# Heads paired as they lie in a fused RWKV and balanced-expert kernel

## The chip, the cores and the metric

The kernel runs on one core of a Trainium2 chip. The metric is device time in microseconds (us), the median of several runs. Before the change it is 385.69 us (three runs, 384.68 to 386.14).

The engines are named as in the profile: PE is TensorE's matmul stream and PEld its weight loads, DVE is VectorE, ACT is ScalarE, POOL is GpSimd, SP is SyncE, which here only issues DMAs.

## The reference

Two blocks run one after the other. The first is an RWKV attention with a decayed state, for 4 batches, 8 heads, 768 steps and 48 dimensions a head:

```
for t in range(S):
    cur = einsum('bhd,bhe->bhde', u * k[t], v[t])
    y[t] = einsum('bhd,bhde->bhe', r[t], state + cur)
    state = w * state + einsum('bhd,bhe->bhde', k[t], v[t])
```

Its output, 3072 tokens of 384 values, goes into a balanced mixture of eight experts. Token and expert pairs are taken in descending order of `x @ w_gate`; each token goes to one expert and each expert takes exactly 384 tokens. Then `out = relu(x @ w1[e]) @ w2[e]`.

## The kernel before

**Rounds.** `Mild.run` (L642) does the attention in 24 rounds. A round n is one batch (B = 4) and one chunk of 128 steps (6 chunks), for all eight heads. Rounds 0 to 3 are the first chunk and have no incoming state; rounds 20 to 23 are the last and leave none. The order on every engine is the order in which the code is written (a manual schedule), so an engine that waits holds up all that stands behind it in its queue.

**What a round does.** k, r and v are loaded by SP (`load`, L331) into rings of five (`krs`) and six (`vts`) slots; k and r come five rounds ahead. In round n:

- `turn(n + 2)`: TensorE transposes k and r of a later round, two heads at a time, into the PSUM banks tagged kT_ps and rT_ps, and VectorE scales them by powers of w into `krT` (L499).
- `own(n + 3)`, `own_sum`, `diagonal(n + 2)`: GpSimd multiplies r, k and u (`rk`), VectorE sums each head to `dd` (L450), ScalarE writes eight diagonal blocks `AT` (L509).
- `pairs(n + 1)`: TensorE forms the products of k and r (`g_ps`, one bank), VectorE places the lower triangle into AT (L526). This is what frees `g_ps`. The text calls it the placing.
- `keep`: TensorE forms the chunk's contribution to the state in the bank "counts" (`kv_ps`, L538), VectorE adds it (L543 or L546), GpSimd decays it (L544). GpSimd's `keys` (L438) makes the keys for it.
- `outputs(n)`: TensorE adds state and chunk parts in `y_ps` (L559), ScalarE copies it to x (L578). In rounds 4, 8, 12, 16 and 20 `gate` and `logits` form four rounds' expert logits, in the bank "few".
- `rows(n - 2)` or `rows_turned` and `rows_out`: x is transposed back to token rows, ScalarE copies them to `xr`, and SP writes them to `x_rows`. `rows` (L621) does eight small transposes into two banks, "few" and "counts"; `rows_turned` (L602) four larger ones into one bank.

**Heads in pairs.** The transposed operands stack two heads on 128 partitions, z = 0 and z = 1. `outputs` puts head h at partition half `h % 2` of its result, so that rows come out in order. Heads 0 to 3 go as (0,1) and (2,3). Heads 4 to 7 go as (5,6) and (7,4): a head of half z then has its result in the other half. For the pair (7,4) to lie side by side, head 4 is copied behind head 7 in `krs`, by `again_one` on ScalarE (L346, two copies a round for rounds 0 to 7) or `again` on VectorE (L342, one for rounds 8 to 23).

**After the rounds.** From round 17 on the early search (`Assignment.early`) runs in eleven steps between the rounds, by a list `steps` of round and place: it picks one expert from the logits of four chunks, then of the fifth, and lists 256 of its tokens (`list_ps`, L1461). GpSimd gathers them (L1550), and TensorE starts with their expert (`e_xT_ps`, `e_h_ps`, `e_o_ps`) while VectorE searches the tokens of the next. Then come the other experts, one after the other. The banks "few" and "counts" belong to the search and are lent to the rounds.

Of the kernel before, what the change touches and what calls it, by code (L numbers as in the profile page):

```python
# [23 lines left out]
T = 128  # L24
PD = 64
# [251 lines left out]
class Mild:  # L277
# [20 lines left out]
    def head(self, a, z):  # L298
        h = 2 * a + z
        return h if h < self.HP else self.HP + (h - self.HP + 1) % self.HP  # L300

    def open(self, ctx):
# [6 lines left out]
        self.krs = const.tile([128, self.NK, 2, H + 2, PD], F32, name="krs")  # L309
# [18 lines left out]
        self.xts, self.live, self.lgs = {}, {}, {}  # L328

    def load(self, n, what):  # L330
# [4 lines left out]
        for x in what:  # L335
            t = self.vts[:, n % self.NV] if x == "v" else self.krs[:, n % self.NK, "kr".index(x)]
            src = {"k": self.k, "r": self.r, "v": self.v}[x]
            nc.sync.dma_start(t[:, 0:H, 0:D], src[b, :, ts(c, T), :].rearrange("h s d -> s h d"))

    def again(self, n):  # L340
        kr, HP, H, D = self.krs[:, n % self.NK], self.HP, self.H, self.D
        self.nc.vector.tensor_copy(kr[:, :, H, 0:D], kr[:, :, HP, 0:D])  # L342

    def again_one(self, n, x):
        t, HP, H, D = self.krs[:, n % self.NK, x], self.HP, self.H, self.D
        self.nc.scalar.copy(t[:, H, 0:D], t[:, HP, 0:D])  # L346

    def start(self):
        nc, HP, H, D = self.nc, self.HP, self.H, self.D
        half = HP // 2  # L350
        nc.vector.memset(self.wp, 1.0)
        with nc.allow_non_contiguous_dma(reason="a row to the partitions"):
            for eng, z, aa, hh in ((nc.sync, 0, slice(0, half), slice(0, HP, 2)),
                                   (nc.scalar, 1, slice(0, half), slice(1, HP, 2)),
                                   (nc.sync, 0, slice(half, HP), slice(HP + 1, H, 2)),
                                   (nc.scalar, 1, slice(half, HP - 1), slice(HP + 2, HP + 3)),
                                   (nc.scalar, 1, slice(HP - 1, HP), slice(HP, HP + 1))):
                eng.dma_start(self.wp[z * PD:z * PD + D, aa], self.w[hh].rearrange("h d -> d h"))
# [17 lines left out]
        nc.gpsimd.memset(self.states, 0.0)  # L376
# [18 lines left out]
        nc.vector.reciprocal(AB[:, 1], AB[:, 0])  # L395
        for x, eng in ((0, nc.gpsimd), (1, nc.vector)):
# [7 lines left out]
    def gate_weights(self):  # L404
        for z in range(2):
            self.nc.sync.dma_start(self.wgp[z * PD:z * PD + self.D, :, 0:self.E],
                                     self.wg.rearrange("(a z d) e -> z d a e", z=2, d=self.D)[z])
# [39 lines left out]

# [80 lines left out]
    def keep(self, n):  # L528
# [3 lines left out]
        if c < C - 1:  # L532
# [9 lines left out]
            if c > 0:  # L542
                nc.vector.tensor_add(S, S, kv)  # L543
                nc.gpsimd.tensor_mul(S, S, wc)  # L544
# [3 lines left out]
    def outputs(self, n, between=None, last=lambda: None):  # L548
# [8 lines left out]
        def add(h, lhsT, rhs, stop):  # L557
            o, q = h // 2, h % 2
# [43 lines left out]
    def rows_turned(self, ns, tag, between=lambda: None):  # L602
        nc, HP = self.nc, self.HP
        shape = [128, len(ns), HP, T]
        ps = (self.walk.ps if tag == "few" else self.ps).tile(shape, F32, name="x_ps", tag=tag)
# [1492 lines left out]
```

## Time and profile before

| what | value |
|---|---|
| median of three runs | 385.69 us |
| the profiled execution's own time | 386.26 us |
| its span, first to last instruction | 384.4 us |
| mean granted clock of TensorE | 0.988 |
| busy: PE, DVE, ACT, POOL | 365.3, 286.8, 180.4, 140.5 us |
| round 5's turn starts | 39.63 us |
| the early expert's first transposes start | 125.45 us |
| first matmul of the next expert | 151.51 us |

All lines come from the profiled execution; times count from the start of its span. A line of the order of time gives start, duration, engine, source line, operation, output and inputs, shapes, and how many instructions were merged. A bracket gives the idle time just before it and what ended that. The granted clock is a share of full speed. A releaser is inferred: where several semaphores were waited for, the profile names one that came late, which need not be the one that the instruction depends on.

### The profile page before, as it was taken

The numbers are of one execution on the slowest core, as the hardware profiler recorded it, in microseconds if no ns is written. First come the engines' busy times: TensorE is split into PE (matmuls) and PEld (weight loads), VectorE is DVE, ScalarE is ACT, GpSimd is POOL, SyncE is SP. The second block draws the span as 40 slices with busy tenths as digits, with TensorE's granted clock in tenths as the row PEclk, the third lists the DMA queues.
The fourth block names the chain that finished last, engine by engine and source line by source line (L and its number), as shares of the span: only waits on it lengthen the run. The fifth ranks groups of instructions, "written<-read, shape, count | busy, mean of one in ns | idle before, by whom it ended". The sixth has DMA issues, their size and how long they took to land. (4 is left out here: it accounts for less than half of the span.)

```text
span 384.4 us, 10425 instructions
## 1 busy us (share of the span) xinstructions
PE 365.3 (95%) x4025; PEld 303.1 (79%) x4025; DVE 286.8 (75%) x963; ACT 180.4 (47%) x470; POOL 140.5 (37%) x174
## 2 busy tenths in 40 slices
PE   8879999999988999999999999999999999999994
PEld 7667878888867765677899799658756989989994
DVE  6875899798995677979679878869457974995730
ACT  4884879878762312225344444322222435535230
POOL 7991999877752004032131231202312213051031
PEclk9997999999999999999999999999999999999998
DMA  7997579987682156474282391507407676391110
GB/s 141 208 188 175 119 169 204 195 186 173 150 322 89 56 179 241 144 260 82 90 341 49 89 377 22 104 2 275 157 20 248 208 211 236 66 366 42 24 62 30
DMA packets 108138, 60.55 MB, mean 158 GB/s; under 512 B 90032, under 2 KB 102320, under 8 KB 108080
## 3 DMA queue, kind: packets, MB, share of 16 engines
q1 hardware_dynamic: 104736, 50.35, 47.9%
q0 software_dynamic: 3104, 9.44, 7.1%
q8 instruction: 34, 0.56, 0.6%
q14 instruction: 24, 0.20, 0.2%
q10 hardware_dynamic: 240, 0.00, 0.0%
HBM read 47.20 MB, written 9.44 MB: 147 GB/s over the span
## 5 line engine op out<-in xcount | busy, mean ns | idle before, releaser
L509 ACT ACTIVATE AT<-ident,dd 128x128 f32<-128x128 f32 x192 | 59.7, 394 | 6.8 <-DVE dd L450 6.8
L1675 PE MATMUL h_ps<-xT,w 128*128 128x384 f32 (+1 forms) x216 | 56.4, 412 | 0.0
L1550 POOL DMA_INDIRECT xg<-x_rows,tok x22 | 22.5, 1024 | 85.8 <-DVE own_c L1476 32.7
L1804 POOL DMA_INDIRECT out_dram<-o_all,to x16 | 19.6, 1225 | 90.6 <-DVE o_all L1792 41.0
L1675 PEld LDWEIGHTS h_ps<-xT,w 128*128 128x128 f32 x216 | 33.3, 191 | 14.3 <-issue 1.9
L526 DVE COPY_PREDICATED AT<-mask,g_ps 64x512 f32<-64x512 uint8 (+1 forms) x48 | 32.3, 723 | 6.5 <-PE g_ps L519 4.3
L1678 ACT ACTIVATE hid<-h_ps 128x384 f32<-128x384 f32 (+1 forms) x32 | 14.0, 437 | 42.6 <-PE h_ps L1675 40.9
L499 DVE TENSOR_TENSOR krT<-kr_ps,W 112x512 f32<-112x512 f32 x44 | 28.1, 678 | 3.6 <-PE kr_ps L495 3.6
L519 PE MATMUL g_ps<-krT 48*64 48x128 f32 (+1 forms) x768 | 27.2, 260 | 2.8 <-DVE AT L526 2.3
L1820 PE MATMUL o_ps<-w,hid 128*128 128x384 f32 x80 | 28.0, 492 | 0.0
L559 PE MATMUL y_ps<-AT,vts 128*64 128x128 f32 x384 | 26.6, 282 | 0.0
L519 PEld LDWEIGHTS g_ps<-krT 48*64 48x64 f32 x768 | 21.3, 136 | 4.9 <-issue 1.5
L445 POOL TENSOR_TENSOR rk<-rk,u_bc 128x384 f32<-128x384 f32 x24 | 24.2, 1007 | 1.9
L444 POOL TENSOR_TENSOR rk<-krs 128x384 f32<-128x384 f32 x24 | 24.5, 1020 | 0.0
L438 POOL TENSOR_TENSOR kss<-krs,wk 128x384 f32<-128x384 f32 x24 | 24.3, 1017 | 0.0
L559 PEld LDWEIGHTS y_ps<-AT,vts 128*64 128x64 f32 x384 | 21.3, 141 | 1.1 <-issue 0.5
L1820 PEld LDWEIGHTS o_ps<-w,hid 128*128 128x128 f32 x80 | 14.5, 190 | 8.0 <-issue 0.6
L1640 ACT ACTIVATE hid<-kept_P 128x384 f32<-128x384 f32 x24 | 12.6, 523 | 17.4 <-DVE kept_P L1644 17.1
L578 ACT COPY x<-y_ps 128x512 f32<-128x512 f32 x24 | 14.0, 583 | 7.4 <-PE y_ps L559 6.6
L495 PE MATMUL kr_ps<-ident,krs 64*112 64x64 f32 x352 | 15.8, 227 | 1.6 <-ACT krs L346 0.9
L495 PEld LDWEIGHTS kr_ps<-ident,krs 64*112 64x112 f32 x352 | 12.2, 134 | 5.7 <-issue 1.4
L1585 ACT COPY xT<-xg 128x768 uint16<-128x768 uint16 x16 | 14.1, 919 | 4.3 <-DMA xg<-xg 4.3
(343 smaller groups left out, 857.8 us busy)
## 6 DMA issues: line engine op xcount, KB each, us to landing
w<-in_moe_w_dram SPq DMA_DIRECT2D x18, 1536.0 KB, 8.6
krs<-in_k_dram SPq DMA_DIRECT2D x24, 192.0 KB, 3.4
krs<-in_r_dram SPq DMA_DIRECT2D x24, 192.0 KB, 3.6
vts<-in_v_dram SPq DMA_DIRECT2D x24, 192.0 KB, 3.8
x_rows<-xr SPq DMA_DIRECT2D x24, 192.0 KB, 3.4
xg<-x_rows,tok POOLq DMA_INDIRECT x22, 5.3
xg<-xg SPq DMA_TRANSPOSE x16, 3.4
out_dram<-o_all,to POOLq DMA_INDIRECT x16, 3.4
```

What stands on the lines that cost most here:

```text
L438: self.nc.gpsimd.tensor_mul(self.kss[:, n % self.NS].rearrange("p (g h) d -> p g h d", g=2)[:, :, :, 0:D], src, self.wk.rearrange("p (g h) ...
L444: nc.gpsimd.tensor_mul(rk, self.krs[:, n % self.NK, 1, 0:H, 0:D], self.krs[:, n % self.NK, 0, 0:H, 0:D])
L445: nc.gpsimd.tensor_mul(rk, rk, self.u_bc)
L495: nc.tensor.transpose(ps[0:P, x, a, :], self.pair(kr[:, x], a)[rows], self.ident[rows, rows])
L499: nc.vector.tensor_mul(t[0:P, :, :, ts(i, PD)], ps[0:P], self.W[0:P, :, :, ts(i, PD)])
L509: nc.scalar.mul(AT[:, z, a, :], self.ident, dd[:, h:h + 1])
L519: nc.tensor.matmul(g_ps[ts(i, PD), z, a, i * PD:], kT[rows, a, ts(i, PD)], rT[rows, a, i * PD:], start=True, stop=True)
L526: nc.vector.copy_predicated(out=AT[keys, :, :, steps], mask=mask, data=g_ps[keys, :, :, steps])
L559: nc.tensor.matmul(yv[q * PD:(q + 1) * PD, o // 2, o % 2, :], lhsT, rhs, start=(o // 2, q) not in seen, stop=stop, skip_group_check=True)
L1550: self.gathered = nc.gpsimd.indirect_dma_start(out=xg[:, c, :], out_offset=None, in_=x_dram[0:within, :], in_offset=bass.IndirectOffsetOnA ...
L1675: nc.tensor.matmul(h_ps[j][:, at], w1[:, f, ts(j, 128)], xT[:, f, at], start=(f == 0), stop=(f == KD - 1))
L1820: nc.tensor.matmul(o_ps, hid[:, j, ts(c, 128)], w2[:, j, :], start=(j == 0), stop=(j == KF - 1))
```

## The change

Heads are paired as they lie: (0,1), (2,3), (4,5), (6,7). The copies of head 4 go, and `krs` has eight head slots instead of ten. The results of heads 4 to 7 are placed crosswise (`place`): an even head of these in the upper partition half, an odd one in the lower. The row copies put them back in order by a strided view (`natural`), and `gate_weights` loads the gate's rows to match, in four DMAs instead of two. w now needs two DMAs on ScalarE's queue instead of three there and two on SP's.

```
     def head(self, a, z):
-        h = 2 * a + z
-        return h if h < self.HP else self.HP + (h - self.HP + 1) % self.HP
+        return 2 * a + z
+
+    def place(self, h):
+        return h // 2, h % 2 if h < self.HP else 1 - h % 2
+
+    def natural(self, xr, q):
+        s = 3 if q else 5
+        return xr[:, q:q + 2 * s].rearrange("p (i s) d -> p i s d", s=s)[:, :, 0:3:2, :]
...
-            for eng, z, aa, hh in ((nc.sync, 0, slice(0, half), slice(0, HP, 2)),
...
-                eng.dma_start(self.wp[z * PD:z * PD + D, aa], self.w[hh].rearrange("h d -> d h"))
+            for z in range(2):
+                nc.scalar.dma_start(self.wp[z * PD:z * PD + D, :], self.w[z:H:2].rearrange("h d -> d h"))
...
         nc.vector.reciprocal(AB[:, 1], AB[:, 0])
+        self.own_raw(0)
...
-                nc.gpsimd.tensor_mul(S, S, wc)
+                self.unscaled.append(lambda: nc.gpsimd.tensor_mul(S, S, wc))
...
+    def row_out(self, n, halves):
+        nc, H, D = self.nc, self.H, self.D
+        xr = self.pool.tile([128, H + 2, D], F32, name="xr", bufs=4)
+        for q, half in enumerate(halves):
+            nc.scalar.copy(self.natural(xr, q), half.rearrange("p (i j) d -> p i j d", i=2))
+        nc.sync.dma_start(self.x_dram[ts(n, 128), :], xr[:, 0:H].rearrange("p h d -> p (h d)"))
...
-                if 1 < n < N - B - 2:
+                if B + 1 < n < N - B - 2:
                     self.rows(n - 2)
-                elif N - B - 2 <= n <= N - B or n == N - 2:
-                    self.rows_out((min(n - 2, N - B - 1),), self.rows_turned((min(n - 2, N - B - 1),), "few"))
+                elif 1 < n < N - 1:
+                    tag = "few" if n <= N - B else "counts" if n == N - B + 1 else "kT_ps"
+                    self.rows_out((n - 2,), self.rows_turned((n - 2,), tag))
...
-            if n < N - 1:
+            if n + 1 < N - B:
                 self.keys(n + 1)
+            while self.unscaled:
+                self.unscaled.pop()()
...
-            steps = [(U - 7, "first"), (U - 7, "paired"), (U - 6, "paired"), (U - 5, "products"), (U - 5, "paired"),
-                     (U - 3, "turning"), (U - 3, "turning"), (U - 3, "states"), (U - 2, "states"),
+            steps = [(U - 7, "first"), (U - 7, "paired"), (U - 6, "paired"), (U - 5, "states"), (U - 4, "paired"),
+                     (U - 4, "last"), (U - 3, "paired"), (U - 2, "products"), (U - 2, "last"),
                      (U - 1, "rows"), (U - 1, "last")]
```

Besides that, the four `keys` of the last chunk go, whose states nobody reads, and the GpSimd scaling of a state is issued one round later. Row blocks 19 and 20 are turned in rounds 21 and 22 in the banks "counts" and kT_ps; before, 19 waited for round 22 and 20 for round 23.

**ScalarE in rounds 0 to 2.** dd sums of round 0 feed the first four diagonals; wk is the table that `keys` reads; x is a round's result. Before:

```order
L424 COPY W<-Q 128x4x62
L346 COPY krs<-krs 128x48
L433 COPY wk<-wk_ps 128x384
L509 ACTIVATE AT<-ident,dd 128x128 x4
L346 COPY krs<-krs 128x48
L509 ACTIVATE AT<-ident,dd 128x128 x4
L346 COPY krs<-krs 128x48
L509 ACTIVATE AT<-ident,dd 128x128 x8
L346 COPY krs<-krs 128x48
L509 ACTIVATE AT<-ident,dd 128x128 x8
```

The same stretch now:

```order
L420 COPY W<-Q 128x4x62
L509 ACTIVATE AT<-ident,dd 128x128 x8
L429 COPY wk<-wk_ps 128x384
L509 ACTIVATE AT<-ident,dd 128x128 x16
L578 COPY x_385<-y_ps 128x512
L509 ACTIVATE AT<-ident,dd 128x128 x4
```

The head copies have gone from between the diagonals, and wk's copy stands behind round 0's eight.

**TensorE at the seam of rounds 2 and 3.** kr_ps are the turns, x_ps the row block, kv_ps the state part. Before:

```order
L627 MATMUL x_ps<-ident,x_396 128x48 x8
L559 MATMUL y_ps<-AT,vts 64x128 x8
L495 MATMUL kr_ps<-ident,krs 112x64 x16
L627 MATMUL x_ps<-ident,x_473 128x48 x8
L538 MATMUL kv_ps<-vts,kss 64x48 x8
```

And now:

```order
L609 MATMUL x_ps<-ident,x_385 128x112 x4
L559 MATMUL y_ps<-AT,vts 64x128 x8
L495 MATMUL kr_ps<-ident,krs 112x64 x16
L609 MATMUL x_ps<-ident,x_460 128x112 x4
L538 MATMUL kv_ps<-vts,kss 64x48 x8
```

The order stays; the row block is four transposes into "few" alone, and kv_ps has "counts" to itself.

**VectorE in rounds 19 and 20.** e_upto to e_hi are the fourth step of the search; the two L526 rows ahead of L543 or behind e_hi are a placing. Before:

```order
L499 TENSOR_TENSOR krT<-kr_ps,W 112x8x64 x2
L1197 SCALAR_TENSOR_TENSOR e_upto<-ones_t,e_st_ps 128x16
L946 TENSOR_TENSOR e_after<-e_upto,e_st_ps 128x16
L1202 SCALAR_TENSOR_TENSOR e_place<-e_after,e_acc 128x16
L1205 TENSOR_SCALAR e_lo<-e_place 128x8
L1208 TENSOR_SCALAR e_hi<-e_place 128x8
L526 COPY_PREDICATED AT<-mask,g_ps 64x8x64
L526 COPY_PREDICATED AT<-mask,g_ps 128x8x64
L946 TENSOR_TENSOR e_row<-e_lo,lo_of 128x512
```

And now:

```order
L499 TENSOR_TENSOR krT<-kr_ps,W 112x8x64 x2
L526 COPY_PREDICATED AT<-mask,g_ps 64x8x64
L526 COPY_PREDICATED AT<-mask,g_ps 128x8x64
L543 TENSOR_TENSOR states<-states,kv_ps 128x4x48
L1189 SCALAR_TENSOR_TENSOR e_upto<-ones_t,e_st_ps 128x16
L938 TENSOR_TENSOR e_after<-e_upto,e_st_ps 128x16
L1194 SCALAR_TENSOR_TENSOR e_place<-e_after,e_acc 128x16
L1197 TENSOR_SCALAR e_lo<-e_place 128x8
L1200 TENSOR_SCALAR e_hi<-e_place 128x8
L451 TENSOR_REDUCE dd<-rk 128x8
```

The search's five operations moved behind the placing and the state's sum; e_row and its two followers come a round later.

More of the change, by code (lines that the diff above doesn't have):

```diff
@@ L308, in open @@
         self.NK, self.NV, self.NS = 5, 6, 3
-        self.krs = const.tile([128, self.NK, 2, H + 2, PD], F32, name="krs")
+        self.krs = const.tile([128, self.NK, 2, H, PD], F32, name="krs")
         self.vts = const.tile([128, self.NV, H, PD], F32, name="vts")
@@ L375, in start @@
         nc.gpsimd.memset(self.vts[:, :, :, D:PD], 0.0)
[L376 removed]
+        nc.gpsimd.memset(self.states[:, :, :, D:PD], 0.0)
         nc.gpsimd.tensor_copy(self.mask, self.mask_f)
@@ L404, in gate_weights @@
     def gate_weights(self):
-        for z in range(2):
-            self.nc.sync.dma_start(self.wgp[z * PD:z * PD + self.D, :, 0:self.E],
-                                     self.wg.rearrange("(a z d) e -> z d a e", z=2, d=self.D)[z])
+        wg = self.wg.rearrange("(i j z d) e -> i z d j e", i=2, z=2, d=self.D)
+        for q in range(2):
+            for i in range(2):
+                self.nc.sync.dma_start(self.wgp[q * PD:q * PD + self.D, 2 * i:2 * i + 2, 0:self.E],
+                                       wg[i, 1 - q if i else q])
     def spread_u(self):
@@ L604, in rows_turned @@
         shape = [128, len(ns), HP, T]
-        ps = (self.walk.ps if tag == "few" else self.ps).tile(shape, F32, name="x_ps", tag=tag)
+        ps = (self.walk.ps if tag in ("few", "counts") else self.ps).tile(shape, F32, name="x_ps", tag=tag)
         P = PD + self.D
@@ L616, in rows_out @@
         for i, n in enumerate(ns):
-            xr = self.pool.tile([128, H, D], F32, name="xr", bufs=4)
-            nc.scalar.copy(xr, ps[:, i].rearrange("p o (z d) -> p (o z) d", z=2)[:, :, 0:D])
-            nc.sync.dma_start(self.x_dram[ts(n, 128), :], xr.rearrange("p h d -> p (h d)"))
+            self.row_out(n, [ps[:, i, :, q * PD:q * PD + D] for q in range(2)])
+    def row_out(self, n, halves):
[4 more added lines that the diff above has]
+        nc.sync.dma_start(self.x_dram[ts(n, 128), :], xr[:, 0:H].rearrange("p h d -> p (h d)"))
     def rows(self, n):
@@ L627, in rows @@
                 nc.tensor.transpose(ps[:, o, :], self.xts[n][at, o, :], self.ident[at, at])
-        xr = self.pool.tile([128, H, D], F32, name="xr", bufs=4)
-        for z, ps in enumerate(halves):
-            nc.scalar.copy(xr.rearrange("p (o z) d -> p o z d", z=2)[:, :, z, :], ps)
-        nc.sync.dma_start(self.x_dram[ts(n, 128), :], xr.rearrange("p h d -> p (h d)"))
+        self.row_out(n, halves)
     def test(self):
@@ L652, in run @@
         self.copy_u(u_ps)
-        self.own(0)
+        self.own_rest(0)
         self.scaled(0, "k", k0, "pieces")
@@ L685, in run @@
                 self.gate_weights()
-            soon, split, full = n <= B, 0 < n < 3, n >= B and n % B == 0
+            split, full = 0 < n < 3, n >= B and n % B == 0
             halves = ((0,), (1,)) if split or full else ((0, 1), ())
@@ L694, in run @@
                 step(n, "first")
-                if not soon and n + 3 < N:
-                    self.again(n + 3)
                 if split:
@@ L730, in run @@
             if n == N - 1:
-                rows = self.rows_turned((N - 4, N - 3), "g_ps", lambda: step(n, "rows"))
-                self.rows_out((N - 4, N - 3), rows)
+                rows = self.rows_turned((N - 3,), "counts", lambda: step(n, "rows"))
+                self.rows_out((N - 3,), rows)
             self.outputs(n, lambda: step(n, "states"), (lambda: self.logits(n // B - 1)) if full else (lambda: None))
```

52 lines of the change are left out of this document (16 added, 36 removed).

## The prediction

> **What bounds the kernel now.** I read the page's first part, then the busy time by stretches, then the order of time of TensorE and of ScalarE in the first 40 us. The page first:
>
> ```profile
> PE 365.3 (95%) x4025; PEld 303.1 (79%) x4025; DVE 286.8 (75%) x963; ACT 180.4 (47%) x470; POOL 140.5 (37%) x174
> ```
>
> TensorE is busy 365.3 of 384.4 us, so the time is TensorE's work plus its waits, and a change of the attention rounds pays only where it shortens a wait, speeds the clock or takes work off TensorE. The stretches show where that is possible (columns: length, then busy time of PE, PEld, DVE, ACT, POOL, granted clock, DMA share, GB/s):
>
> ```profile
> 23.70:27.10 3.40, 1.85 (x38) 1.35 (x34) 3.12 (x6) 3.40 (x14) 3.25 (x7) 1.00 0.86 180
> 27.10:33.92 6.82, 6.34 (x88) 5.46 (x88) 2.62 (x6) 3.52 (x13) 3.08 (x4) 0.50 0.96 203
> 39.63:91.67 52.04, 50.79 (x1353) 44.11 (x1352) 46.10 (x105) 42.70 (x138) 44.92 (x68) 1.00 0.79 174
> 91.67:125.45 33.78, 30.75 (x663) 25.12 (x663) 27.79 (x82) 20.43 (x60) 17.27 (x19) 1.00 0.63 188
> 148.97:360.00 211.03, 209.03 (x1200) 171.77 (x1201) 162.49 (x612) 80.17 (x153) 42.24 (x38) 1.00 0.49 157
> ```
>
> From 148.97 on the experts keep TensorE busy for 209.03 of 211.03 us: whatever ends earlier before that moves the end by as much. The middle rounds (5 to 16) lose 1.25 of 52.04 us, the late rounds 3.03 of 33.78. The opening is the loose stretch: from 27.10 to 33.92 the clock is granted at 0.50, right after 3.40 us in which TensorE had work for only 1.85. Its waits there, in order of time (the bracket is the wait and what ended it):
>
> ```profile
> 13.40 0.27 PE L495 MATMUL kr_ps<-ident,krs 64*112 64x64 f32 x2 [0.86 <-ACT krs L346]
> 14.75 1.10 PE L519 MATMUL g_ps<-krT 48*64 48x128 f32 x32 [0.60 <-DVE AT L526]
> 17.65 1.10 PE L519 MATMUL g_ps<-krT 48*64 48x128 f32 x32 [0.32 <-DVE AT L526]
> 21.44 1.10 PE L519 MATMUL g_ps<-krT 48*64 48x128 f32 x32 [0.53 <-DVE krT L499]
> 24.68 0.27 PE L495 MATMUL kr_ps<-ident,krs 64*112 64x64 f32 x1 [0.29 <-DVE krT L499]
> 25.28 0.66 PE L495 MATMUL kr_ps<-ident,krs 64*112 64x64 f32 x15 [0.33 <-DVE krT L499]
> 27.58 1.10 PE L538 MATMUL kv_ps<-vts,kss 128*64 128x48 f32 x16 [1.41 <-ACT krs L346]
> 34.64 0.67 PE L538 MATMUL kv_ps<-vts,kss 128*64 128x48 f32 x16 [0.72 <-ACT krs L346]
> ```
>
> The eight waits sum to 5.06 us. The last two name a head copy (L346), which kv_ps doesn't read. ScalarE's order there gives the real releaser:
>
> ```profile
> 25.26 0.59 ACT L578 COPY x<-y_ps 128x512 f32<-128x512 f32 x1
> 25.73 1.28 ACT L509 ACTIVATE AT<-ident,dd 128x128 f32<-128x128 f32 x4
> 26.91 0.52 ACT L630 COPY xr<-x_ps 128x192 f32<-128x192 f32 x2
> 27.32 0.25 ACT L346 COPY krs<-krs 128x48 f32<-128x48 f32 x1
> ```
>
> kv_ps lives in the bank "counts", which the second row copy (L630) empties at 26.91 + 0.52 = 27.43; 0.15 later kv_ps starts. The row copy is late because ScalarE did x and four diagonals first.
>
> **The opening.** Head copies and order first.
>
> ```profile
> 9.46 0.69 DVE L477 TENSOR_TENSOR krT<-kT_ps,W 112x512 f32<-112x512 f32 x1 [0.53 <-PE kT_ps L460]
> 10.06 0.54 DVE L450 TENSOR_REDUCE dd<-rk 128x8 f32<-128x384 f32 x1
> 11.76 0.45 DVE L675 TENSOR_TENSOR chunk<-ones 128x4 f32<-128x4 f32 x1
> 10.64 1.28 ACT L509 ACTIVATE AT<-ident,dd 128x128 f32<-128x128 f32 x4
> 13.26 1.35 DVE L526 COPY_PREDICATED AT<-mask,g_ps 64x512 f32<-64x512 uint8 x2 [1.05 <-ACT AT L509]
> L346 ACT COPY krs<-krs x16: 217/228/246, 4.8 to 35.7; 128x48 f32<-128x48 f32 x16
> ```
>
> Sixteen ScalarE copies of about 0.23 us go, 3.6 in all. dd of round 0 stands ahead of round 1's scaling (9.46, before which VectorE idled 0.53) and uses that gap, so it is there near 9.5 instead of 10.6. Eight diagonals (two groups of 1.28) then end near 12.0, and VectorE, free at 11.76 + 0.45 = 12.2, starts its first placing about 1.05 earlier than 13.26. The wait of 0.86 at 13.40 ends with its copy; what is late next is g_ps, still held by that placing, so round 1's products start near 13.7 instead of 14.75, and the lead of a microsecond holds to round 3. wk's copy, behind the diagonals now, is wanted by GpSimd's keys, which have two rounds' products queued ahead of them: nothing, or up to 0.5 at kv_ps of round 0 if they are short. own(0) is split in two, and its first product stands ahead of Q on GpSimd; the r it reads is loaded earlier, because two loads of w leave SP's queue, so I price it at nothing; were r late, Q and the first scaling would wait for at most that product, a microsecond.
>
> Then the bank. Rows of rounds 0 to 3 use "few" alone, so kv_ps no longer waits for the row copy: 1.41 and 0.72 go. The price is on TensorE:
>
> ```profile
> 25.72 0.45 PE L627 MATMUL x_ps<-ident,x 48*128 48x48 f32 x8
> 96.36 0.60 PE L609 MATMUL x_ps<-ident,x 112*128 112x112 f32 x4
> ```
>
> 0.15 us more in each of four rounds, 0.6 in all. Two row copies stay two, so ScalarE pays nothing.
>
> Last the clock. With those waits gone I place TensorE from 20 to 27 us with under a microsecond of idle in any 3.4 us, against 1.55 in 23.70 to 27.10, and so expect no fall. The 6.34 us of work done at 0.50 would take half: 3.2 less; I take 2.9, since loads and hand-overs don't halve. Sum of the opening: 5.06 of waits plus 2.9 of clock, less about 2.0 of waits that stay (0.7 before round 1's products, 0.3 and 0.5 before rounds 2 and 3, 0.4 at the fifth turn, each for VectorE), less 0.6: 5.4. Bounds: 2.5 if the clock still falls, 6.2 if the waits that stay halve.
>
> The load of w (five DMAs on two queues, now two on ScalarE's) sets the powers:
>
> ```profile
> 4.36 0.49 DVE L391 TENSOR_SCALAR ones<-wp 128x4 f32<-128x4 f32 x1 [1.56 <-DMA wp<-in_w_dram]
> ```
>
> One ScalarE issue fewer may land it 0.4 earlier, the longer transfers 0.4 later. TensorE runs without a wait to 12.5 either way: nothing. Two more DMAs for wgp delay SP by about a microsecond in round 2, behind loads that are five rounds ahead: nothing.
>
> **The middle rounds.** VectorE loses one copy a round:
>
> ```profile
> 52.31 0.45 PE L627 MATMUL x_ps<-ident,x 48*128 48x48 f32 x7 [0.63 <-DVE states L543]
> 86.90 0.45 PE L627 MATMUL x_ps<-ident,x 48*128 48x48 f32 x7 [0.53 <-DVE states L543]
> L342 DVE COPY krs<-krs x16: 186/202/879, 39.0 to 107.5; 128x96 f32<-128x96 f32 x16
> ```
>
> Both waits are for a VectorE that is behind. A copy of the median takes 0.20 us, some of it beside its neighbours, the longest 0.88. Four copies precede the first wait (I take 0.5 of its 0.63), long ones the second (I take 0.4 of 0.53). I take 0.9; bounds 0.3 and 1.16. Scaling the states later on GpSimd costs nothing: they are read four rounds on.
>
> **The late rounds.** Steps of the early search move between rounds 19 and 23.
>
> ```profile
> 103.39 0.17 DVE L1197 TENSOR_TENSOR_SCAN e_upto<-ones_t,e_st_ps 128x16 f32<-128x16 f32 x1
> 105.31 1.31 DVE L526 COPY_PREDICATED AT<-mask,g_ps 64x512 f32<-64x512 uint8 x2
> 106.77 1.10 PE L519 MATMUL g_ps<-krT 48*64 48x128 f32 x32 [1.35 <-DVE AT L526]
> 116.44 0.60 PE L609 MATMUL x_ps<-ident,x 112*128 112x112 f32 x4 [1.48 <-DVE e_after L946]
> 120.11 0.17 PE L1461 MATMUL list_ps<-e_both,alike 128*128 128x8 f16 x1
> 122.39 0.95 POOL L1550 DMA_INDIRECT xg<-x_rows,e_tok  x1 [0.30 <-issue]
> 126.34 0.55 PE L1917 MATMUL e_xT_ps<-ident,xg 128*128 128x128 f32 x3 [0.40 <-DMA xg<-x_rows,e_tok]
> ```
>
> Today 1.92 us of search (103.39 to 105.31) stand ahead of a placing, and TensorE waits 1.35; moved behind it, that wait goes. The 1.48 goes because row 20 takes another bank. But VectorE's work is the same and is nearly the bound here, so waits return: by its durations about 0.9 at the first e_some_ps, which now has its vectors built just before, about 1.0 at list_ps, whose e_both follows round 23's placing, which now has the fifth chunk's search right ahead of it, 0.2 at row 18, and 0.4 more at e_xT_ps, since fewer transposes lie between list_ps and it (126.34 - 120.11 = 6.2 us of landing must be covered). 2.83 less 2.5, plus 0.5 from four VectorE copies that go: 0.8. Bounds: 2.8 if VectorE isn't late, and a loss of 1.0 if both new waits are twice as long.
>
> **Sum.** 5.4 + 0.9 + 0.8 = 7.1. The profiled execution took 386.26 us (its span 384.4 and 1.9 around it), which gives 379.2; the median of the runs shown is 0.57 lower. I forecast 379.2.
>
> **The rivals.** One: the clock falls all the same, because it is the kind of work, not the waits. Between 23.70 and 27.10 about 1.2 of the 1.85 busy us are transposes (the rows at 24.68, 25.28 and 25.72), and the turns and rows stay, 0.15 longer each. For it: no single wait was longer than 1.41. Against it:
>
> ```profile
> 5.76 1.10 PE L460 MATMUL kT_ps<-ident,krs 128*112 128x128 f32 x4
> 10.05 0.60 PE L460 MATMUL rT_ps<-ident,krs 128*112 128x128 f32 x4
> ```
>
> TensorE became about twice as fast near 10 us after four microseconds of nothing but transposes. The price is the 2.9: 382.1. [...]
>
> Two: the late rounds give back what they gain and 1.0 more, by list_ps and e_xT_ps; 381.0. For it: VectorE is busy 27.79 of 33.78 there.
>
> Three: the loads become the bound of rounds 5 to 9, which come 5 us sooner.
>
> ```profile
> vts<-in_v_dram SPq DMA_DIRECT2D x24, 192.0 KB, 3.8
> ```
>
> A middle round (52.04 / 12 = 4.3 us) moves k, r, v and a row block, four times 192 KB, so 181 GB/s, and at a share of 0.96 the engines moved 203: a tenth in hand. Of the 5.4 I would lose up to 2 until the loads, five rounds ahead, have caught up: 381.2.
>
> Four, slower than before: the early token list comes so late that TensorE idles at e_xT_ps, and the clock falls on top of it. A wait W there costs W + 2.9 once W is over about 1.5; from W = 4.2 the gain is eaten, from 6.1 it is slower by over 0.5%. At W = 7 it gives 389.1. For it: the list's landing ends in a wait of 0.40 already. Against it: my chain for the list adds under a microsecond.
>
> **How the numbers follow.** Forecast 0.60, the clock 0.20, late rounds 0.10, loads 0.05, slower 0.05. The range 377.0 to 383.0 holds the first four singly (the low end: opening 6.2, middle 1.1, late 1.9), and leaves out the fourth rival, two rivals together and some luck below: about 0.16. Within 0.5% (1.9 us, what a measurement can tell) lies only a pair of rivals: 0.06; faster 0.89, slower 0.05.
>
> **What would show it.** Right: no stretch at 0.50 after 12 us; no wait of kv_ps in rounds 3 and 4; round 5's turn near 34 instead of 39.63; no wait before the products of round 21. Wrong: a clock of 0.50 anywhere in the rounds, waits over 2 us at list_ps or e_xT_ps, or an expert stretch that isn't as long as now.

## The result and the profile after

The changed kernel takes 378.79 us (median of four executions, 378.08 to 379.35) against 385.19 for the kernel before (four, 384.44 to 386.14): a ratio of 0.9832, 95% interval 0.9801 to 0.9862. The forecast was 379.2. The profiled execution took 378.61 us, its span 376.8 where it was 384.4: 7.6 less, forecast 7.1.

The page's first part, and the busy time by stretches (length, busy time of PE, PEld, DVE, ACT, POOL, granted clock, DMA share, GB/s). The first two stretches are the ones shown of before; the third reaches from round 5's turn to round 17's, the fourth on to the first token transposes, the last is the experts'.

```profile
PE 361.9 (96%) x4009; PEld 300.3 (80%) x4009; DVE 281.6 (75%) x947; ACT 178.6 (47%) x462; POOL 136.0 (36%) x170
```

```profile
23.70:27.10 3.40, 3.07 (x74) 2.46 (x70) 2.79 (x6) 3.40 (x13) 3.25 (x8) 1.00 0.68 143
27.10:33.92 6.82, 6.82 (x168) 5.67 (x165) 5.13 (x12) 5.58 (x19) 6.59 (x11) 1.00 1.04 226
34.42:85.67 51.25, 50.85 (x1349) 44.15 (x1348) 43.74 (x93) 42.62 (x138) 44.10 (x63) 1.00 0.85 187
85.67:117.41 31.74, 30.45 (x664) 25.08 (x664) 25.41 (x78) 20.94 (x66) 10.51 (x12) 1.00 0.67 201
140.88:352.00 211.12, 208.86 (x1201) 171.92 (x1202) 162.42 (x612) 80.12 (x153) 42.25 (x38) 1.00 0.49 157
```

The stretch from 27.10 to 33.92 ran at 0.50 before and now at 1.00, with 168 matmuls where there were 88; the 3.40 us ahead of it hold 3.07 us of work, not 1.85. GpSimd is down from 17.27 to 10.51 us in the late rounds: remember this for later.

TensorE's order of time: its waits in the opening, with the two kv_ps that waited 1.41 and 0.72 before.

```profile
4.85 1.61 PE L407 MATMUL u_ps<-u_row,one_row 1*128 1x384 f32 x2 [0.60 <-DMA u_row<-in_u_dram]
...
12.93 0.55 PE L416 MATMUL unread_ps<-ident 128*128 128x128 f32 x3 [0.58 <-ACT wk L429]
14.04 1.10 PE L519 MATMUL g_ps<-krT 48*64 48x128 f32 x32 [0.56 <-DVE AT L526]
...
16.92 1.10 PE L519 MATMUL g_ps<-krT 48*64 48x128 f32 x32 [0.31 <-DVE AT L526]
...
20.72 1.10 PE L519 MATMUL g_ps<-krT 48*64 48x128 f32 x32 [0.64 <-DVE krT L499]
24.53 0.66 PE L495 MATMUL kr_ps<-ident,krs 64*112 64x64 f32 x15 [0.33 <-DVE krT L499]
25.65 0.67 PE L538 MATMUL kv_ps<-vts,kss 128*64 128x48 f32 x16
29.43 0.67 PE L538 MATMUL kv_ps<-vts,kss 128*64 128x48 f32 x16
```

And its waits from round 5 to the token list:

```profile
47.07 0.45 PE L632 MATMUL x_ps<-ident,x 48*128 48x48 f32 x7 [0.31 <-DVE states L543]
...
103.59 0.25 PE L1220 MATMUL e_some_ps<-e_vals,e_row 128*128 128x32 f16 x4 [0.27 <-ACT LG L600]
...
112.34 0.18 PE L1453 MATMUL list_ps<-e_both,alike 128*128 128x8 f16 x1 [1.02 <-DVE e_both L938]
```

The three unread_ps at 12.93 are transposes that nobody reads, put there by `idle`; what they wait for is their bank, which the copy of wk empties. kv_ps follows the row transposes without a bracket. Of the waits of 0.63, 0.53, 1.35 and 1.48 behind round 5, one of 0.31 is left, and two are new.

The same places in the profiled execution of every kernel that was run (us; the columns between are differences of starts in TensorE's order of time; a fall is a stretch at a granted clock of 0.50 within the rounds):

| kernel | round 5's turn | to round 17's turn | from there to the first e_h_ps | span | falls |
|---|---|---|---|---|---|
| before | 39.63 | 52.04 | 35.05 | 384.4 | 27.10, 6.83 long |
| after | 34.42 | 51.25 | 32.63 | 376.8 | none |
| bank_alone | 36.35 | 52.29 | 37.81 | 383.8 | 14.86, 3.41; 113.85, 6.83 |
| fill_10 | 36.85 | 52.00 | 34.90 | 380.7 | none |
| two_banks | 38.69 | 51.19 | 32.88 | 381.4 | 26.31, 6.83 |
| copies_back | 34.58 | 51.98 | 33.01 | 378.1 | none |
| after_again | 34.68 | 51.26 | 32.64 | 376.7 | none |
| old_steps | 35.02 | 51.47 | 31.86 | 376.5 | none |
| old_late_banks | 35.36 | 51.43 | 33.19 | 377.8 | 14.72, 3.41 |
| list_later | 34.63 | 51.23 | 32.45 | 376.6 | none |
| keys_back | 33.84 | 51.96 | 34.01 | 378.7 | none |
| late_old | 34.44 | 51.26 | 36.36 | 381.3 | 101.92, 3.41 |
| w_two_queues | 34.24 | 52.39 | 32.93 | 378.1 | none |
| old_steps_w | 33.43 | 55.14 | 32.68 | 380.5 | 49.04, 3.41 |

So the opening gained 5.21, the middle 0.79, the late rounds 2.42, together 8.42. The rest gives 0.8 back: the last expert's first matmul (half_ps) comes 247.42 after the first e_h_ps (247.02 before), and the span ends 11.1 behind it (10.7).

The mean clock differs from execution to execution of the same kernel (0.983 to 1.000 in the 42 of before named below). A stretch of 3.41 us at 0.50 lowers an execution's mean clock by 0.0044. The traces of before and after have one more stretch at 0.50 at their very end, from 382.08 and 374.74, behind TensorE's last work (379.11 and 371.09): 2.4 and 2.1 us of the span. By an estimate from the mean clocks of the other twelve profiled executions, less their falls, the last stretch covers about 0.4 to 3.9 us in them and lowers the mean by up to 0.005, so a mean of 0.995 alone does not say whether there was a fall within the rounds. Of 45 executions of before, taken beside the experiments, the three slowest (388.8 to 391.6 us) were in a slow state and are left out; the other 42 have a median clock of 0.990, and ten of the changed kernel 0.994 to 1.000.

### The profile page after: what moved, and what is told of

Same layout as the page of the kernel before. It is cut to its first block, busy times and chain, and to the rows that moved or that the text cites. A ratio compares the mean times of both kernels' runs of the same rounds, so it can differ in the third digit from the quotient of the medians.

```text
span 376.8 us, 10340 instructions
## 1 busy us (share of the span) xinstructions
PE 361.9 (96%) x4009; PEld 300.3 (80%) x4009; DVE 281.6 (75%) x947; ACT 178.6 (47%) x462; POOL 136.0 (36%) x170
## 5 line engine op out<-in xcount | busy, mean ns | idle before, releaser
L526 DVE COPY_PREDICATED AT<-mask,g_ps 64x512 f32<-64x512 uint8 (+1 forms) x48 | 32.4, 724 | 4.2 <-PE g_ps L519 3.2
L519 PE MATMUL g_ps<-krT 48*64 48x128 f32 (+1 forms) x768 | 26.3, 255 | 1.5 <-DVE AT L526 0.9
L559 PE MATMUL y_ps<-AT,vts 128*64 128x128 f32 x384 | 25.7, 276 | 0.0
L433 POOL TENSOR_TENSOR kss<-krs,wk 128x384 f32<-128x384 f32 x20 | 20.4, 1020 | 0.0
L623 ACT COPY xr<-x_ps 128x192 f32<-128x192 f32 x48 | 12.9, 323 | 7.5 <-PE x_ps L609 4.5
L1775 PE MATMUL p_ps<-W,H 128*128 128x128 f32 x128 | 15.3, 275 | 0.0
L559 PE MATMUL y_ps<-krT,states 48*64 48x128 f32 x320 | 15.2, 278 | 0.0
```

Of the source, the lines that this page charges most:

```text
L433: self.nc.gpsimd.tensor_mul(self.kss[:, n % self.NS, :, 0:D], self.krs[:, n % self.NK, 0, :, 0:D], self.wk)
L519: nc.tensor.matmul(g_ps[ts(i, PD), z, a, i * PD:], kT[rows, a, ts(i, PD)], rT[rows, a, i * PD:], start=True, stop=True)
L526: nc.vector.copy_predicated(out=AT[keys, :, :, steps], mask=mask, data=g_ps[keys, :, :, steps])
L559: nc.tensor.matmul(yv[q * PD:(q + 1) * PD, o // 2, o % 2, :], lhsT, rhs, start=(o // 2, q) not in seen, stop=stop, skip_group_check=True)
```

## Experiments

Two theories stood at the start. Mine: idle time of TensorE makes the clock fall, and the change removes it by the banks (opening), the copies (middle) and the order of the steps (late). The rival: the clock falls for the kind of work, transposes above all.

**fill_10: only work is added.** The kernel before, with ten transposes that nobody reads in the gap ahead of round 3's kv_ps:

```
+                if n == 3:
+                    self.idle(10, "g_ps")
                 if n <= B:
                     self.keep(n - 1)
```

> The kernel before with ten transposes that nobody reads (128x128, 1.3 us at full clock) put ahead of round 3's kv_ps, where TensorE waited 1.41 us: no wait is shortened, work is only added. Theory (idle time makes the clock fall, and transposes count as work): no stretch at 0.50, the 6.34 us done there take 3.2 less: 382.0 us. Rival (transposes don't count as work for the clock): the stretch at 0.50 stays: 385.2 us, or more if the added work is in the way.

Measured: 382.87 us against 385.74, ratio 0.9946 (0.9921 to 0.9971). TensorE's order there, and two stretches, the second of which ran at 0.50 before:

```profile
26.10 1.31 PE L420 MATMUL unread_ps<-ident 128*128 128x128 f32 x10
27.59 0.67 PE L538 MATMUL kv_ps<-vts,kss 128*64 128x48 f32 x16 [0.18 <-ACT krs L346]
```

```profile
23.68:27.10 3.42, 2.80 (x47) 2.37 (x44) 3.15 (x6) 3.42 (x14) 3.23 (x6) 1.00 0.89 186
27.10:30.51 3.41, 3.23 (x75) 2.62 (x75) 1.15 (x4) 3.08 (x13) 3.26 (x6) 1.00 0.99 214
```

kv_ps starts where it did (27.59, before 27.58), so the gap is filled and nothing comes earlier by it, and yet round 5's turn comes 2.78 us earlier, because the clock stays at 1.00. Useless work made the kernel faster, and that work was transposes. The rival falls.

**bank_alone: one part of the change on the kernel before.**

```
-                if 1 < n < N - B - 2:
+                if 1 < n <= B + 1:
+                    self.rows_out((n - 2,), self.rows_turned((n - 2,), "few"))
+                elif 1 < n < N - B - 2:
```

> The kernel before with one part of the change: rows of rounds 0 to 3 turned whole into bank "few", so that kv_ps finds "counts" free. Head copies, order of the opening and late rounds stay as before. Theory (gaps in TensorE's work make the clock fall): the waits 1.41 and 0.72 at kv_ps go, no stretch at a granted clock of 0.50 follows, four row turns are 0.15 us dearer: 385.2 - 2.1 - 2.9 + 0.6 = 380.8 us. Rival (the kind of work makes the clock fall, transposes being most of what TensorE does there): the waits go, the stretch at 0.50 stays: 385.2 - 2.1 + 0.6 = 383.7 us.

Measured: 385.82 us, ratio 0.999 (0.9958 to 1.0022): nothing, where I expected 4.4. The profiled execution reaches round 5's turn 3.28 us earlier than before and has lost it again by the first e_h_ps. Two things stand out in it. First, the next wait moves in, for a head copy that a transpose does read:

```profile
30.63 0.27 PE L495 MATMUL kr_ps<-ident,krs 64*112 64x64 f32 x2 [0.64 <-ACT krs L346]
```

Second, the clock falls elsewhere: at 14.86, behind the opening's waits, and at 113.85, behind the late wait of 1.48:

```profile
110.44:113.85 3.41, 1.67 (x22) 1.36 (x22) 3.31 (x11) 0.93 (x3) 0.00 (x0) 1.00 0.13 42
113.85:117.27 3.42, 3.42 (x55) 2.94 (x55) 1.60 (x5) 0.48 (x1) 0.00 (x0) 0.50 0.16 58
```

The falls are not the whole of it. Two of the twelve executions have a clock of 0.997, and they took 382.61 and 383.02 us; the executions of before with 0.996 or more took 383.2 on average. So without falls the bank alone is worth about 0.4.

**two_banks: that part undone on the changed kernel.**

```
-                if B + 1 < n < N - B - 2:
+                if 1 < n < N - B - 2:
```

> The changed kernel with the bank part undone: rows of rounds 0 to 3 go through the two banks "few" and "counts" again; all else as changed. Theory: kv_ps of rounds 3 and 4 waits for the row copies again, about 1.2 us (from 25.65 to 26.23 + 0.52 + 0.15 = 26.9) and 0.5 us; with the 0.33 ahead of it that is 1.5 us idle within 3.4, as in the kernel before, so the clock falls to 0.50 for a while: 378.8 + 1.7 - 0.6 + 2.9 = 382.8 us. Rival (the fall before came of the longer series of waits since 13 us, most of which stay gone): two waits, no fall: 379.9 us.

Measured: 381.96 us, ratio to before 0.9896 (0.9860 to 0.9932), where the changed kernel has 0.9832. Both waits and the fall are back:

```profile
26.64 1.09 PE L538 MATMUL kv_ps<-vts,kss 128*64 128x48 f32 x16 [1.16 <-POOL by_digit L852]
33.70 0.67 PE L538 MATMUL kv_ps<-vts,kss 128*64 128x48 f32 x16 [0.72 <-ACT xr L623]
```

```profile
22.90:26.32 3.42, 1.96 (x40) 1.46 (x36) 3.17 (x6) 3.42 (x13) 3.34 (x6) 1.00 0.74 142
26.32:29.73 3.41, 3.09 (x50) 2.70 (x52) 0.56 (x2) 2.52 (x9) 3.26 (x6) 0.50 1.04 225
```

(The profile names by_digit for the first and xr, a row copy, for the second; for the first too I take it to be the row copy, as before.) The fall is that of the profiled execution; of the seven, two have a mean clock under 0.99. So the banks are worth about 2 us once the copies are gone (2.5 by the ratio of the changed kernel, 1.7 by that of its repetition, after_again), and about 0.4 while they are there. The parts are not additive, and each was priced in the forecast as if the other were in place.

**copies_back: the copies' own time.** The changed kernel, head copies at their old places into a spare tile that nobody reads:

```
+                if n > B and n + 3 < N:
+                    self.again(n + 3)     # VectorE: spare <- krs
...
+            if n <= B:
+                self.again_one(n + 3, 0)  # ScalarE: spare <- krs
```

> The changed kernel with the head copies added again at their old places (twelve or so on ScalarE in the opening, one a round on VectorE later), into a spare tile that nobody reads: the time of the copies alone, without the dependence of transposes on them. Theory (the copies cost because both engines are late there): about 0.5 in the opening and 0.8 in the middle and 0.2 late: 380.3 us, with the waits of 0.6 and 0.5 for VectorE near rounds 8 and 16 back. Rival (engines other than TensorE have room, and the middle rounds gained by the states' scaling moved on GpSimd): 378.8 us.

Measured: 380.77 us, ratio 0.9871 (0.9835 to 0.9908), near the 380.3 of the theory. The middle is 0.73 longer, and its two waits are back:

```profile
47.54 0.45 PE L641 MATMUL x_ps<-ident,x 48*128 48x48 f32 x7 [0.62 <-DVE states L552]
81.80 0.45 PE L641 MATMUL x_ps<-ident,x 48*128 48x48 f32 x7 [0.20 <-DVE states L552]
```

The late stretch is 0.38 longer, and the opening only 0.16. By this run, what the copies cost in the opening was that transposes read them, and not ScalarE's time.

**after_again: the changed kernel, more executions.**

> The changed kernel once more, beside the next three on the same chip, with more executions. The granted clock of each execution tells how much of it ran at 0.50. Theory (a fall of the clock is an event that some executions have, wherever a window of about 3.4 us holds too much idle time, and the change removes its three places near 15, 26 and 115 us): nearly every execution at 0.994 or above, 379 us, spread under 1.5 us. Rival (the one profile without a fall was chance): a third or more of the executions below 0.993, up to 3 us longer.

Measured: 379.10 us (378.26 to 379.58), ratio 0.9852 (0.9823 to 0.9881); all six executions have a clock of 0.995 or more. The theory held.

**old_steps and old_late_banks: what carries the late gain?** The first puts the list `steps` back, the second rows 19 to 21:

```
-            steps = [(U - 7, "first"), (U - 7, "paired"), (U - 6, "paired"), (U - 5, "states"), (U - 4, "paired"),
-                     (U - 4, "last"), (U - 3, "paired"), (U - 2, "products"), (U - 2, "last"),
+            steps = [(U - 7, "first"), (U - 7, "paired"), (U - 6, "paired"), (U - 5, "products"), (U - 5, "paired"),
+                     (U - 3, "turning"), (U - 3, "turning"), (U - 3, "states"), (U - 2, "states"),
```

```
...
-                rows = self.rows_turned((N - 3,), "counts", lambda: step(n, "rows"))
+                rows = self.rows_turned((N - 4, N - 3), "g_ps", lambda: step(n, "rows"))
...
```

> The changed kernel with the early search's steps at their old places in rounds 19 to 23; rows keep their new banks. Theory A (the order of the steps carries the late gain): the wait of 1.35 before round 21's products returns, the new ones of 0.27 and 1.02 go or shrink, but VectorE does the search ahead of a placing again and list_ps comes late by up to a microsecond: 1.0 to 1.5 more, 380.1 us. Theory B (the banks carry it): within 0.5 of the changed kernel, 379.2 us.

> The changed kernel with rows 19 to 21 at their old places and banks (row 19 in round 22, rows 20 and 21 together at the end in "g_ps"); the steps stay at their new places. Theory A (the order of the steps carries the late gain): within 0.5 of the changed kernel, 379.2 us. Theory B (the banks carry it): a wait of about 1.5 for "few" at a row's transposes, as the one of 1.48 before: 380.3 us.

Measured: old_steps 378.48 us (378.02 to 379.05), ratio 0.9837 (0.9809 to 0.9865); old_late_banks 379.00 us, 0.9849 (0.9822 to 0.9877). Neither takes the gain away, so both theories fall. With the old steps the wait of 1.35 before round 21's products does not come back,

```profile
100.43 1.10 PE L519 MATMUL g_ps<-krT 48*64 48x128 f32 x32 [0.18 <-DVE AT L526]
```

nor does list_ps wait, and the late stretch is shorter than in the changed kernel (31.86 against 32.63 and 32.64). By the times the two can't be told apart; by the trace, the new order of the steps costs 0.8. With the old banks the stretch is 0.56 longer: a row's transposes wait 1.04 for their bank again (at 112.59, for VectorE's e_some) and the first tokens come 0.77 late, while list_ps does not wait.

**A third theory.** Comparing VectorE before and after at the search's small operations shows where the gain is. Before, VectorE and GpSimd:

```profile
103.79 0.56 DVE L1202 SCALAR_TENSOR_TENSOR e_place<-e_after,e_acc 128x16 int16<-128x16 f32 x1
104.39 0.93 DVE L1205 TENSOR_SCALAR e_lo<-e_place 128x8 int32<-128x8 int32 x1
```

```profile
103.32 1.00 POOL L445 TENSOR_TENSOR rk<-rk,u_bc 128x384 f32<-128x384 f32 x1
104.28 1.02 POOL L438 TENSOR_TENSOR kss<-krs,wk 128x384 f32<-128x384 f32 x1
```

After, where GpSimd has nothing from 99.0 to 113.2:

```profile
98.75 0.28 DVE L1194 SCALAR_TENSOR_TENSOR e_place<-e_after,e_acc 128x16 int16<-128x16 f32 x1
99.06 0.17 DVE L1197 TENSOR_SCALAR e_lo<-e_place 128x8 int32<-128x8 int32 x1
```

e_lo, eight elements a partition, took 0.93 us and ended at 105.32; GpSimd's product ended at 105.30. e_place took 0.56 and ended at 104.35, the product ahead of it at 104.32. After, with no product beside them, they took 0.28 and 0.17. Both ended with the product that ran beside them. The change takes four of these products away, the keys of the last four units.

**keys_back: these products again, nothing else.**

```
-            if n + 1 < N - B:
+            if n < N - 1:
                 self.keys(n + 1)
```

> The changed kernel with GpSimd's products of the last four units' keys (kss, 1.01 us each, which nothing reads) done again, as the kernel before did; nothing else differs. Theory (some small VectorE operations last until the GpSimd product that runs beside them ends: before, e_lo took 0.93 from 104.39 and the product ended at 105.30): one or two of e_place, e_lo, e_eq take 0.6 to 0.9 again instead of 0.17 to 0.28, the waits at e_some_ps and list_ps grow, 0.8 to 1.5 more: 380.2 us. Rival (GpSimd's work lies beside the rest): 379.1 us as the changed kernel.

Measured: 380.63 us, ratio 0.9842 (0.9814 to 0.9869), which by itself does not differ from the changed kernel. In the trace the late stretch is 34.01 us, 1.38 more. VectorE, GpSimd and TensorE there:

```profile
93.81 0.83 DVE L1241 TENSOR_SCALAR e_less<-e_cnt 128x8 f32<-128x8 f32 x1
...
100.10 1.06 DVE L1200 TENSOR_SCALAR e_hi<-e_place 128x8 int32<-128x8 int32 x1
```

```profile
93.60 1.02 POOL L433 TENSOR_TENSOR kss<-krs,wk 128x384 f32<-128x384 f32 x1
...
100.11 2.00 POOL L433 TENSOR_TENSOR kss<-krs,wk 128x384 f32<-128x384 f32 x2
```

```profile
99.59 0.60 PE L609 MATMUL x_ps<-ident,x 112*128 112x112 f32 x4 [0.60 <-DVE e_after L938]
...
104.81 0.27 PE L1220 MATMUL e_some_ps<-e_vals,e_row 128*128 128x32 f16 x4 [0.70 <-DVE e_vals L938]
```

e_less ends with the product beside it (94.64 and 94.62), and e_hi takes 1.06 where it took 0.17. The longer operations show in the trace; the price of 1.38 is that of one execution. The edit touches neither the opening nor the middle, and yet the first is 0.6 shorter in this execution and the second 0.7 longer (there GpSimd waits 0.60 for r), so a price read from one trace can be off by that much. The time of the whole kernel does not confirm it: the profiled span is 1.9 us longer than the changed kernel's, but the ratio is the same, because this run, late_old, w_two_queues and old_steps_w were on a chip on which the kernel before took 386.89 us. These four are best compared by their ratios.

**late_old: all three late edits undone.** The diffs of old_steps, old_late_banks and keys_back together.

> The changed kernel with all of the late part undone: old places of the search's steps, old places and banks of rows 19 to 21, the last keys on GpSimd again; opening and middle rounds as changed, no head copies. Theory (late rounds are bound by VectorE, and any one of the three late edits is enough to hide what the others would hide): waits of 1.3 and 1.5 are back, 2.0 to 2.4 more: 381.3 us. Rival (the late gain came from the four head copies that left VectorE): 379.6 us, both waits under 0.8.

Measured: 383.03 us, ratio 0.9899 (0.9870 to 0.9928). The waits are back, and the longer one brings the clock down:

```profile
101.05 1.20 PE L519 MATMUL g_ps<-krT 48*64 48x128 f32 x32 [1.60 <-DVE AT L526]
...
111.35 0.60 PE L609 MATMUL x_ps<-ident,x 112*128 112x112 f32 x4 [1.24 <-DVE e_after L939]
```

```profile
98.51:101.92 3.41, 1.81 (x52) 1.55 (x46) 3.34 (x10) 1.48 (x5) 1.07 (x2) 1.00 1.01 369
101.92:105.33 3.41, 3.41 (x55) 2.34 (x52) 3.29 (x6) 2.43 (x9) 2.47 (x3) 0.50 1.04 404
```

The late stretch is 3.73 us longer. Of that I put 1.7 to the window at 0.50, an estimate (half of its 3.41 us of work), which fits the mean clock of 0.992 or 0.993 in five of the six executions; 2.0 are waits. One undone edit costs 1.38, 0.56 or minus 0.77, all three together 2.0 and a fall. With the 0.38 that the head copies cost the late stretch in copies_back, this makes up the gain of 2.42.

**list_later: a wait of the changed kernel filled.**

```
-                     (U - 1, "rows"), (U - 1, "last")]
+                     (U - 1, "states"), (U - 1, "last")]
```

> The changed kernel with list_ps one place later: behind the last round's 16 products with the states (0.60 us) instead of ahead of them, on TensorE alone. Theory (TensorE waits 1.02 for e_both there, and could do the 0.60 meanwhile; the token gathers land in time all the same): 0.6 less, 378.2 us. Rival (the tokens' landing is the next thing waited for, as the 0.40 at e_xT_ps was before): the wait moves to e_xT_ps, 378.8 us.

Measured: 378.38 us (377.89 to 378.68), ratio 0.9833 (0.9805 to 0.9861). The 1.02 at list_ps goes, and 0.59 of it appears at the tokens:

```profile
117.93 0.55 PE L1909 MATMUL e_xT_ps<-ident,xg 128*128 128x128 f32 x3 [0.59 <-DMA xg<-x_rows,e_tok]
```

Late stretch 32.45 against 32.64: mostly the rival. The median is 0.7 lower, which six executions each don't settle.

**w_two_queues and old_steps_w: the load of w.**

```
-                nc.scalar.dma_start(self.wp[z * PD:z * PD + D, :], self.w[z:H:2].rearrange("h d -> d h"))
+                (nc.sync, nc.scalar)[z].dma_start(self.wp[z * PD:z * PD + D, :], self.w[z:H:2].rearrange("h d -> d h"))
```

The second has the old `steps` as well.

> The changed kernel with the first of its two loads of w issued by SP ahead of the loads of k and r, the second by ScalarE as before. Theory (both on ScalarE, the second behind the first, land 0.34 late, at 4.70, and the powers, the first placing and round 1's products follow, 14.04 instead of the 13.7 that the prediction had): w lands near 4.4, round 1's products start near 13.75, 378.8 us. Rival (the landing waits for the loads of k and r that share the DMA engines, or SP's loads come later by one issue and dd of round 0 with them): 379.1 us or 0.2 more.

> The changed kernel with the search's steps at their old places, as in the run where that alone took 0.6 off, and with w loaded on two queues. Theory: both add up, 378.2 us, no wait over 0.35 behind round 5. Rival (the 0.6 was the chance of one set of executions): 379.0 us.

Measured: w_two_queues 379.50 us, ratio 0.9814 (0.9789 to 0.9839); old_steps_w 379.08 us (377.96 to 382.19), 0.9798 (0.9770 to 0.9826). By the ratios both may be a little faster than the changed kernel, but the intervals overlap, and I count neither as shown. The traces show why the step is no plain gain. VectorE reads w at 3.25 instead of 4.70, but round 1's products start at 13.85 instead of 14.04; and SP has a load of w ahead of its first load of k, which delays that by an estimated 0.5 us (before, with two ahead of it, it was issued at 1.90, in the changed kernel, with none, at 0.81). GpSimd, VectorE and TensorE of w_two_queues:

```profile
32.02 1.01 POOL L442 TENSOR_TENSOR rk<-krs 128x384 f32<-128x384 f32 x1 [1.13 <-DMA krs<-in_r_dram]
```

```profile
43.38 1.00 DVE L892 TENSOR_SCALAR first_e<-iota 128x8 f32<-128x8 f32 x1
```

```profile
48.04 0.44 PE L632 MATMUL x_ps<-ident,x 48*128 48x48 f32 x7 [0.84 <-DVE states L543]
```

GpSimd waits 1.13 for r, its products slide onto VectorE's small operations (first_e takes 1.00; in the changed kernel 0.23), VectorE is late, TensorE waits, and the middle is 1.14 longer. The same chain, with 1.11 for r, gives old_steps_w a wait of 1.12 at 46.32, and the clock falls at 49.04. That the later issue makes r late is not shown: in keys_back, where w is loaded as in the changed kernel, GpSimd waits for r too, 0.60.

No version was shown to beat the changed kernel; old_steps and list_later, 378.5 and 378.4, are the candidates.

## Why the prediction was right, and where it was not

**The clock: right.** Forecast 2.9 for the stretch at 0.50; fill_10, which does nothing else, has 2.78. The limit that the fourth rival used, a wait of about 1.5, was close too: in the traces a fall followed windows with 1.45 us or more of idle time, and none with 1.35 or less (see the last section). But the forecast treated the fall as a fixed part of the kernel. It is an event that a given execution has or not. In six of the 42 executions of before the clock is 0.996 or more, and these took 382.67 to 383.92 us, mean 383.2. The ten of the changed kernel have a median of 379.0. So about 4.2 of the gain are shorter waits, and the rest of the distance from before's median in those 42 (385.7) is falls that became rarer.

**The opening: right in sum (5.4, measured 5.2), wrong in how its parts depend on each other.** The 1.41 and 0.72 for the bank were priced by themselves; in bank_alone, where a head copy holds up the next transposes, about 0.4 of them is left, and two_banks shows their price with the copies gone. The first placing moved from 13.26 to 12.55, by 0.71, not 1.05, and round 1's products from 14.75 to 14.04, not 13.7. The step that failed is "TensorE runs without a wait to 12.5 either way: nothing", said of the loads. u lands 3.1 us after its issue, before 2.2, and so TensorE has its new wait of 0.60 at 4.85. What stands behind it there is late by as much: r of round 0 is transposed at 7.71 instead of 7.08, and VectorE's scaling of it follows. Before and after:

```profile
8.18 0.75 DVE L475 TENSOR_TENSOR krT<-rT_ps,Q 112x264 f32<-112x264 f32 x2 [0.28 <-PE rT_ps L460]
```

```profile
8.81 0.76 DVE L475 TENSOR_TENSOR krT<-rT_ps,Q 112x264 f32<-112x264 f32 x2
```

So dd of round 0 is there at 10.03 and not near 9.5, and the eight diagonals end at 12.51 and not near 12.0. The wait for u goes with the place of SP's first load of k: it is 0 in before and fill_10, where two loads of w stand ahead of that on SP (issued at 1.90 before), 0.37 and 0.42 in old_steps_w and w_two_queues, with one ahead, and 0.58 to 0.64 in after, keys_back, late_old, copies_back and two_banks, with none (issued at 0.81 in after). w itself lands later too, but does no harm: VectorE reads it at 4.70 instead of 4.36, and the next operation starts at 4.91 where it was 4.89.

A second term priced at nothing was nearly as late: own(0), whose first product now stands ahead of Q on GpSimd. It was feared for a late r; it held up VectorE instead. VectorE and GpSimd after:

```profile
4.91 0.96 DVE L376 TENSOR_TENSOR ones<-ones 128x4 f32<-128x4 f32 x1
```

```profile
4.85 0.99 POOL L442 TENSOR_TENSOR rk<-krs 128x384 f32<-128x384 f32 x1 [0.42 <-DMA krs<-in_r_dram]
```

This first product of the powers of w took 0.20 before; now it ends at 5.87, where GpSimd's product ends at 5.84, and the powers' reciprocal starts at 6.92 instead of 6.14. That is hidden behind the wait for u, but only just, and it shows why w_two_queues won so little: w is read at 3.25 there and the reciprocal starts at 6.33, but the scaling of r waits 0.46 for TensorE, and round 1's products gain 0.2.

**The middle: right.** Forecast 0.9, measured 0.79, and copies_back gives 0.73 of it back, at the two places named.

**The late rounds: the wrong reason and a third of the size (0.8, measured 2.4).** Two steps failed. "moved behind it, that wait goes": the 1.35 goes in old_steps too, without the move. "VectorE's work is the same": the instructions are, their durations are not (e_lo took 0.17 us instead of 0.93). The four keys that go were known, but the sum has no term for them; what they cost was VectorE's time. Of the new waits, list_ps came out as forecast (1.0, measured 1.02); e_some_ps waits 0.27, not 0.9, since its vectors are ready sooner.

**What nobody forecast:** the 0.8 that is given back behind the rounds. Half is a wait that before did not have, for the tokens of a later expert:

```profile
263.92 1.05 PE L1557 MATMUL xT_ps<-ident,xg 128*128 128x128 f32 x6 [0.46 <-DMA xg<-x_rows,tok]
```

The other half is the landing of the last output rows: the span ends 4.8 us after that DMA's issue on GpSimd (372.04), before 4.4 (380.06). after_again has no such token wait and gives back 0.4 instead of 0.8 (247.15 and 10.9), so the landing of DMAs differs between executions by this much, and I don't put it down to the change.

**The total: near, and in part by luck.** The span is 7.6 shorter and the forecast had 7.1, but the late rounds gave 1.6 more than priced, and half of that went again in a loss behind the rounds that nobody priced. By the medians the gain is 6.4.

**The rivals.** The first fell by fill_10, the second did not happen, the fourth neither (the longest wait is 1.02). The third, the loads as the next bound, is not seen in the changed kernel, but in keys_back, w_two_queues and old_steps_w, whose round 5 starts only 0.2 to 1.0 earlier: GpSimd waits 0.60, 1.13 and 1.11 for r. It was closer than its chance of 0.05 said.

## What to carry to other kernels

Price a removed wait together with what is late next: the freed bank was worth about 0.4 us while head copies held up the next transposes, and about two once they were gone. Where TensorE idles for two fifths of some 3.4 us, add up the idle time along the whole neighbourhood: in these traces 1.45 us or more of 3.41 was followed by a fall of the clock, and the fall behind the 1.55 us of before cost 2.78 by fill_10. There ten unneeded matmuls in the gap were cheaper than the gap (382.87 us against 385.74). Work of an engine that nobody waits for can lie beside longer operations on another: in the late rounds VectorE's e_lo took 0.93 us beside a GpSimd product and 0.17 without one. Look at small operations whose duration varies, and at what ends when they end.

## What the runs showed of the hardware

**The clock in these traces.** The seven falls within the rounds, in six of the 14 traces, are 3.41 or 6.83 us long, and in the trace of before the full clock ahead of the fall lasts 17.07 (10.03 to 27.10), five times 3.41. So I laid a grid of 3.41 us over each trace from its first full clock, which comes at 4.48 to 11.98, and added up TensorE's idle time in each window up to 150 us. Seven windows had 1.45 us or more (1.45, 1.48, 1.55, 1.60, 1.74, 1.88, 1.95), and every one was followed by a window or two at 0.50. None with less was; the largest were 1.35, 1.24, 1.24, 1.22 and 1.21. This is the window of 1.35, in fill_10, whose next window is at 1.00 again:

```profile
102.14:105.56 3.42, 2.07 (x57) 1.72 (x60) 3.38 (x11) 0.91 (x3) 1.05 (x3) 1.00 1.07 397
```

So in these traces a fall came with 1.45 us of idle time in a window and not with 1.35; TensorE had worked for 1.47 to 1.96 us in the windows ahead of a fall. Why the clock falls is not shown. The grid lies differently from execution to execution, which fits the record: the kernel before, with its wait of 1.41, has a mean clock of 0.996 or more in six of its 42 executions and less in the others. Behind the first full clock, the most idle windows of the changed kernel's two traces had 0.64 and 0.80.

**VectorE beside GpSimd.** Some small VectorE operations took 0.56 to 1.06 us instead of 0.14 to 0.28 when a GpSimd product ran beside them, and those followed up ended within 0.05 us of a product's end: e_place and e_lo of the kernel before (0.56 and 0.93, ended 104.35 and 105.32, the products 104.32 and 105.30), e_less of keys_back (0.83, 94.64 and 94.62), the first product of the powers after (0.96, 5.87 and 5.84) and first_e of w_two_queues (1.00, 44.38 and 44.34). Why, no run shows. Not every operation took longer: a reduction beside a product kept its time (e_m of the kernel before, 0.18 at 111.69, with kss from 110.19 to 113.15), and so did e_upto and e_after, which read a result of TensorE (0.17 each, from 103.39, with rk from 103.32 to 104.32).
